# A retention layer with a gated feed-forward on one core: order of the first chunk, place of a weight load, and a split of the first four blocks

## The chip, the cores and the metric

One core of a Trainium2 chip runs the whole program. The metric is device time in microseconds, the median over several executions; less is better. The kernel before took 257.64 us (median of 11, 255.73 to 260.2).

## The reference

Two layers follow each other. The first is retention, a linear attention with a decay per head; the second is an RMS norm and a SwiGLU feed-forward over the tokens.

```python
# q, k, v: (4, 8, 768, 64) float32
gamma = 1.0 - 2.0 ** (-5.0 - np.arange(H))
for t in range(S):
    state = gamma[None, :, None, None] * state + einsum('bhd,bhe->bhde', k[:, :, t], v[:, :, t])
    y[:, :, t] = scale * einsum('bhd,bhde->bhe', q[:, :, t], state)
x = y.transpose(0, 2, 1, 3).reshape(B * S, H * D)          # 3072 tokens x 512
rms = np.sqrt(np.mean(x * x, axis=-1, keepdims=True) + 1e-06)
xn = x / rms * rms_g
g = xn @ w_gate                                            # 512 x 1536
silu = g * (1.0 / (1.0 + np.exp(-g)))
out = silu * (xn @ w_val) @ w_out                          # 1536 x 512
```

## The kernel before

The 768 positions are cut into six chunks of 128 (`c`), and a chunk holds all four batches (`b`): 512 tokens. Per chunk there are an attention part and a feed-forward part. All heads of a batch are worked on together, two heads to a group of 128 rows. Matmuls take bf16 and sum in float32. The decay is put into v (`vdec`) and into the output (`ydec`), so that the state is a plain sum.

**Attention of one batch of a chunk**, in pieces that are placed one by one:

- `cast` (POOL): q and k to bf16, v times decay to `vp`. For chunks 2 to 5 two transposing DMAs on SP (`qT`, `kT`) follow at once.
- T, `piece_t` (chunks 0 and 1): eight transposes on TensorE into `qk_ps`, and one ScalarE copy to `qkT`.
- A, `piece_a`: eight matmuls into two `a_ps` (k against q), and on VectorE the causal mask into `am`, in two halves.
- Y, `piece_y`: `am` times `vp` into `y_ps`, from chunk 1 on the state (`st_b`) times q added to it, and k times `vp` into `kv_ps`; VectorE scales to `x`, ScalarE sums the squares (`xsq`), POOL makes `rstd`. From chunk 1 on VectorE adds `kv_ps` to the state `st_f` and POOL casts it to `st_b`, in two halves of 64 rows. In chunk 0 ScalarE copies it (S, `piece_s`) and POOL casts it in the feed-forward slots 0 to 3 (`piece_sb`).
- N, `piece_n`: VectorE makes `xn`; for chunks 2 to 5 one more transposing DMA on SP writes `xnT`.
- X, `piece_x` (chunks 0 and 1): four transposes on TensorE, and the product with the norm's weight, on ScalarE or VectorE, into `xnT`.

**Feed-forward of a chunk**, in slots: twelve blocks `gv(n)` of eight matmuls of 512 columns (gate and value), a Silu on ScalarE (`sg`) and a product on VectorE (`hT`); then the down projection. In chunk 0 that is twelve quarter slots (`down(b, 4i, 4i+4)`), of which the first four need the first piece of `wo_b` alone, the next four the second, the last four the third; in later chunks four slots of twelve matmuls. ScalarE copies the sum to `o_sb` (three buffers), and SP writes it out.

**What sets the order.** The program is scheduled by hand: each engine and each DMA queue runs in program order. Chunk 0's attention is one written string of steps (lines 374 to 382), with the gate and value weights (W0 to W3) loaded between them on POOL. After that, while chunk c's feed-forward runs, the attention of chunk c+1 is hung into its slots by `PLAN` (chunks 2 to 5) and `PLAN1` (chunk 1): in each slot first the block or down, then the pieces that the plan lists for it, by batch.

Transfers: chunk 0's batch 0 comes over SP, batches 1 to 3 over POOL's queue with a cast on the way (`load0`). Chunk 1's twelve loads stand on SP behind the landing of W1. The three pieces of `wo_b` are issued on POOL ahead of slots 9 (two) and 12. At slot 16 of chunk 0 SP gets the norm's weight (`g_bc`) and the twelve loads of chunk 2, the first of them behind the landing of the second `wo_b` piece:

```python
    WS = {9: (0, 1), 12: (2,)}
...
            if c == 0 and i == 16:
                nc.sync.dma_start(out=g_bc, in_=moe_rms_g.partition_broadcast(128))
                for b in range(B):
                    load(2, b, after=landed["wo", 1])
```

Chunk 0's four outputs are issued on SP after these (slots 20 to 23), and the transposes of chunk 2 after the outputs.

PSUM is split into four banks for attention (`aps`) and four for the feed-forward (`fps`); chunk 0's four `kv_ps` lie in `fps` until S has copied them. Between chunk 0's attention and the feed-forward stand six matmuls without use (`hot`), which keep TensorE busy.

Of the kernel before, what the change touches and what calls it, by code (L numbers as in the profile page):

```python
# [9 lines left out]
F32 = mybir.dt.float32  # L10
BF16 = mybir.dt.bfloat16
AX = mybir.AxisListType
AF = mybir.ActivationFunctionType
ALU = mybir.AluOpType
# [3 lines left out]
def kernel(  # L18
# [77 lines left out]
    for h in range(H):  # L96
# [17 lines left out]
    nc.scalar.activation(warm, zero, AF.Silu)  # L114
    mhalf = const.tile([128, 1], F32, name="mhalf")
    nc.vector.memset(mhalf, -0.5)
    load0(1)
    ident = const.tile([128, 128], BF16, name="ident")
    make_identity(nc, ident)
    load0(2)  # L120
    causal = const.tile([128, 128], BF16, name="causal")
    nc.gpsimd.memset(causal, 1.0)
    nc.gpsimd.affine_select(
        out=causal, in_=causal, compare_op=ALU.is_ge, fill=0.0, base=0,
        pattern=[[1, 128]], channel_multiplier=-1)
    load0(3)

    g_bc = const.tile([128, DM], F32, name="g_bc")


    st_f = [const.tile([128, NHP, D], F32, name=f"st_f{b}") for b in range(B)]
    st_b = [const.tile([128, NHP, 2 * D], BF16, name=f"st_b{b}") for b in range(B)]
    for b in range(B):
        nc.vector.memset(st_b[b], 0.0)
# [55 lines left out]
    def piece_t(c, b):  # L190
        if c > 1:
            return
        if c == 0:
            cur[c, b] = dict(qb=raw0["qb", b], kb=raw0["kb", b])
        d = cur[c, b]
        qk_ps = aps.tile([128, 2, NHP, 128], BF16, name="qk_ps", tag="at")
        for i, n in enumerate(("qb", "kb")):
            for hp in range(NHP):
                nc.tensor.transpose(qk_ps[:, i, hp, :], d[n][:, hp * 128:(hp + 1) * 128], ident)
        qkT = work.tile([128, 2, NHP, 128], BF16, name="qkT")  # L200
        nc.scalar.copy(qkT, qk_ps)
        d["qT"] = qkT[:, 0]
        d["kT"] = qkT[:, 1]

# [15 lines left out]
    def piece_y(c, b):  # L220
# [31 lines left out]
        if c == 0:  # L252
            d["kv"] = kv_ps
        elif c < NCH - 1:
            for i in range(2):
                r = slice(i * 64, i * 64 + 64)
                kv = kv_ps[r, :, i * 64:i * 64 + 64]
                nc.vector.tensor_tensor(out=st_f[b][r], in0=st_f[b][r], in1=kv, op=ALU.add)  # L258
                nc.gpsimd.tensor_copy(st_b[b][r, :, i * 64:i * 64 + 64], st_f[b][r])  # L259

    def piece_s(b):
        for i in range(2):
            r = slice(i * 64, i * 64 + 64)
            nc.scalar.copy(st_f[b][r], cur[0, b]["kv"][r, :, i * 64:i * 64 + 64])

    def piece_sb(b):
        for i in range(2):
            r = slice(i * 64, i * 64 + 64)
            nc.gpsimd.tensor_copy(st_b[b][r, :, i * 64:i * 64 + 64], st_f[b][r])

    def piece_rstd(c, b):
        ms = work.tile([128, 1], F32, name="ms")
# [18 lines left out]
    def piece_x(c, b):  # L291
        d = cur[c, b] if c == 0 else cur.pop((c, b))
        if c > 1:
            return
        xn = d["xn"]
        xt_ps = aps.tile([128, KS, 128], BF16, name="xt_ps", tag="at")
        for s in range(KS):
            nc.tensor.transpose(xt_ps[:, s, :], xn[:, s * 128:(s + 1) * 128], ident)
        if c == 0 and b < B - 1:
            for s in range(KS):  # L300
                nc.scalar.activation(cur[c, "xnT"][:, s, b * C:(b + 1) * C], xt_ps[:, s, :],
                                     AF.Copy, scale=g_col[:, s:s + 1])
            return
        nc.vector.tensor_tensor(  # L304
            out=cur[c, "xnT"][:, :, b * C:(b + 1) * C], in0=xt_ps,
            in1=g_col[:, :, None].to_broadcast([128, KS, 128]), op=ALU.mult)
# [2 lines left out]
        cur[c, "xnT"] = work.tile([128, KS, GT], BF16, name="xnT", bufs=2)  # L309


    PLAN = dict(cast=(0, 1, 2, 3), t=(1, 3, 5, 7), a=(4, 6, 8, 10), y=(5, 7, 9, 11), n=(7, 9, 11, 13), x=(8, 10, 12, 14))

    PLAN1 = dict(cast=(5, 6, 8, 11), t=(7, 9, 11, 17), a=(8, 10, 13, 18), y=(9, 11, 15, 20), n=(11, 13, 17, 22), x=(12, 15, 19, 23))

    def attention(c):
        s = [[] for _ in range(24 if c == 1 else 16)]
# [7 lines left out]


    def ffn(c):
        xnT = cur.pop((c, "xnT"))
        hT = ffw.tile([128, NFF, GT], BF16, name="hT", bufs=2)
        slots = []  # L330

        def gv(n):
            sl = slice(n * 128, (n + 1) * 128)
            g_ps = fps.tile([128, GT], F32, name="g_ps", tag="ff")
            for s in range(KS):
                nc.tensor.matmul(g_ps, wg_b[:, s, sl], xnT[:, s, :], start=s == 0, stop=s == KS - 1)  # L336
            v_ps = fps.tile([128, GT], F32, name="v_ps", tag="ff")
            for s in range(KS):
                nc.tensor.matmul(v_ps, wv_b[:, s, sl], xnT[:, s, :], start=s == 0, stop=s == KS - 1)  # L339
            sg = ffw.tile([128, GT], BF16, name="sg")  # L340
            nc.scalar.activation(sg, g_ps, AF.Silu)  # L341
            nc.vector.tensor_tensor(out=hT[:, n, :], in0=sg, in1=v_ps, op=ALU.mult)  # L342

        o_t = {}

        def down(b, n0=0, n1=NFF):
            if n0 == 0:
                o_t[b] = fps.tile([128, DM], F32, name="o_ps", tag="ff")
            o_ps = o_t[b]
            for n in range(n0, n1):  # L350
                nc.tensor.matmul(o_ps, hT[:, n, b * C:(b + 1) * C], wo_b[:, n, :],  # L351
                                 start=n == 0, stop=n == NFF - 1)
            if n1 < NFF:
                return
            o_sb = ffw.tile([128, DM], F32, name="o_sb")
            nc.scalar.copy(o_sb, o_ps)  # L356
            nc.sync.dma_start(out=out_v[c, b], in_=o_sb)

        for n in range(NFF):
            slots.append(lambda n=n: gv(n))  # L360
        if c == 0:
            for i in range(3):
                for b in range(B):
                    slots.append(lambda b=b, i=i: down(b, 4 * i, 4 * i + 4))
        else:
            for b in range(B):
                slots.append(lambda b=b: down(b))
        return slots


    begin(0)
    P = dict(C=lambda c, b: piece_c(b), V=lambda c, b: piece_v(b), S=lambda c, b: piece_s(b),
             T=piece_t, A=piece_a, Y=piece_y, N=piece_n, X=piece_x, W=lambda c, i: load_w(i))
    for step in ("C0 T0 V0 W0 A0 T1 V1 Y0 W1 A1 T2 V2 N0 Y1 W2 X0 A2 T3 V3 N1 Y2 W3 X1 A3 N2 Y3 X2 S0 S1").split():
        P[step[0]](0, int(step[1]))
    hot = aps.tile([128, GT], F32, name="hot", tag="at")
    for i in range(6):
        nc.tensor.matmul(hot, ident, cur[0, 3]["qT"].rearrange("p a b -> p (a b)"), start=True, stop=True)
    piece_s(2)
    piece_s(3)  # L380
    piece_n(0, 3)
    piece_x(0, 3)
    for b in range(B):
        load(1, b, after=landed["w", 1] if b == 0 else None)

    WS = {9: (0, 1), 12: (2,)}
    for c in range(NCH):
        f_slots = ffn(c)
        a_slots = attention(c + 1) if c + 1 < NCH else [[] for _ in range(16)]
        for i, f_slot in enumerate(f_slots):  # L390
            if c == 0:
                for j in WS.get(i, ()):
                    load_wo(j)
            f_slot()
            if c == 0 and i < B:
                piece_sb(i)
            if c == 0 and i == 16:
                nc.sync.dma_start(out=g_bc, in_=moe_rms_g.partition_broadcast(128))
                for b in range(B):
                    load(2, b, after=landed["wo", 1])  # L400
            if 0 < c < NCH - 2 and i in (5, 7, 9, 11):
                load(c + 2, (i - 5) // 2)
            for f in a_slots[i]:
# [29 lines left out]
```

## Time and profile before

| | us |
|---|---|
| median of 11 runs | 257.64 (255.73 to 260.2) |
| the profiled execution's own time | 258.51 |
| its span, first to last instruction | 256.8 |
| TensorE busy | 228.2 (89% of the span) |
| VectorE busy | 128.1 (50%) |
| POOL busy | 95.5 (37%) |
| ScalarE busy | 90.1 (35%) |
| first feed-forward matmul of chunk 0 | 24.66 |
| first feed-forward matmul of chunk 1 | 69.34 |

PE is TensorE (PEld its weight loads), DVE is VectorE, ACT is ScalarE, POOL is GpSimd, SP the engine whose queue issues most transfers; a name with q behind it (SPq) is that engine's sequencer or DMA queue. A row of the timeline has the start in us, the length, the engine, the line of the kernel, the operation, output and inputs by their names in the program, and in brackets how long the engine had been idle before it and what ended the wait. Rows of neighbouring instructions of one kind are merged (x4): the length is then from the first start to the last end. A matmul's recorded length reaches into the next one's, so prices are taken from start to start.

### The profile page before, as it was taken

To read this page: it belongs to the slowest core of one execution; us is meant where nothing else is said; L and a number is where in the kernel's file an instruction comes from. 1 tells how busy PE (TensorE), PEld (TensorE's weight loads), DVE (VectorE), ACT (ScalarE), POOL (GpSimd) and SP (SyncE) were. 2 spreads that over 40 slices of the span, in tenths; PEclk is the share of its full clock that TensorE was granted. 3 is DMA by queue.
4 is the path that set the end of the run, shared out by engine and by line. 5 is a ranking of instruction groups with operands and counts; after the bars stand their busy time and mean duration, and the time that the engine had idled before them with its cause. 6 is when DMAs were issued, how large, how long until landed. Compare 5 with 4: busy or idle time off the path is not lost.

```text
span 256.8 us, 4122 instructions
## 1 busy us (share of the span) xinstructions
PE 228.2 (89%) x1483; PEld 111.2 (43%) x1510; DVE 128.1 (50%) x227; ACT 90.1 (35%) x178; POOL 95.5 (37%) x177
## 2 busy tenths in 40 slices
PE   1767999696859999999999999999999999999993
PEld 0543445353424544444544444444444444444441
DVE  3793336764423898125888036896045772143300
ACT  6477333512322323233243133432333322333221
POOL 8968156372590222960224930244911111000000
PEclk9997999999988999999999999999999999999999
DMA  9999999979984599945999545999354112300022
GB/s 135 180 199 203 204 221 210 147 151 203 224 240 86 122 221 172 204 123 102 156 223 196 145 103 105 192 216 190 102 123 84 20 20 83 125 0 1 0 84 82
DMA packets 108069, 35.94 MB, mean 140 GB/s; under 512 B 99024, under 2 KB 104656, under 8 KB 108048
## 3 DMA queue, kind: packets, MB, share of 16 engines
q1 hardware_dynamic: 95232, 29.37, 58.6%
q0 software_dynamic: 12288, 6.29, 18.4%
q8 instruction: 12, 0.20, 0.3%
q14 instruction: 9, 0.07, 0.2%
q10 hardware_dynamic: 528, 0.00, 0.1%
HBM read 28.58 MB, written 6.29 MB: 136 GB/s over the span
## 4 chain that ended last, share of the span: by engine, by line
PE 64%; DVE 15%; DMA 7%; ACT 5%; issue 4%; POOL 2%; SPq 1%; ACTq 0%; DVEq 0%; POOLq 0%
PE o_ps L351 20%; PE v_ps L339 19%; PE g_ps L336 18%; DVE am L215 5%; DVE hT L342 4%; DMA wo_b<-in_moe_w_out_dram 3%; DMA v_f<-in_v_dram 2%; DVE x L243 2%; ACT sg L341 2%; ACT xsq L247 2%; PE y_ps L228 2%; DMA out_dram<-o_sb 2%; PE a_ps L211 1%; DVE xn L284 1%; DVE xn L288 1%
## 5 line engine op out<-in xcount | busy, mean ns | idle before, releaser
L342 DVE TENSOR_TENSOR hT<-sg,v_ps 128x512 bf16<-128x512 bf16 x72 | 49.4, 687 | 92.0 <-PE v_ps L339 75.0
L339 PE MATMUL v_ps<-xnT,wv_b 128*128 128x512 bf16 x282 | 74.3, 383 | 3.1 <-ACT o_sb L356 2.6
L336 PE MATMUL g_ps<-xnT,wg_b 128*128 128x512 bf16 x275 | 73.6, 383 | 2.1 <-DVE xnT L304 1.7
L351 PE MATMUL o_ps<-wo_b,hT 128*128 128x512 bf16 x281 | 63.8, 379 | 3.8 <-DMA wo_b<-in_moe_w_out_dram 3.3
L341 ACT ACTIVATE sg<-g_ps 128x512 bf16<-128x512 f32 x72 | 42.7, 594 | 58.6 <-PE g_ps L336 55.5
L339 PEld LDWEIGHTS <-wv_b 128*128 128x128 bf16 x288 | 28.4, 99 | 37.4 <-issue 4.1
L273 POOL TENSOR_SCALAR ms<-ssq 128x1 f32<-128x1 f32 x24 | 4.6, 191 | 102.6 <-ACT xsq L247 102.5
L351 PEld LDWEIGHTS <-hT 128*128 128x128 bf16 x288 | 27.6, 98 | 34.9 <-issue 1.8
L336 PEld LDWEIGHTS <-wg_b 128*128 128x128 bf16 x288 | 26.2, 98 | 30.6 <-issue 2.2
L247 ACT ACTIVATE xsq<-x 128x512 f32<-128x512 f32 x24 | 15.1, 630 | 50.7 <-DVE x L243 48.6
L215 DVE TENSOR_TENSOR am<-a_ps,causal 128x512 bf16<-128x512 f32 x48 | 30.8, 683 | 1.5 <-PE a_ps L211 1.3
L356 ACT COPY o_sb<-o_ps 128x512 f32<-128x512 f32 x24 | 14.0, 585 | 47.2 <-PE o_ps L351 38.7
L180 POOL TENSOR_TENSOR vp<-v_f,vdec 128x512 bf16<-128x512 f32 x20 | 20.8, 1038 | 1.4 <-DMA v_f<-in_v_dram 1.4
L228 PE MATMUL y_ps<-vp,am 128*128 128x64 bf16 x192 | 13.1, 198 | 6.1 <-DVE am L215 6.0
L243 DVE TENSOR_TENSOR x<-y_ps,ydec 128x512 f32<-128x512 f32 x24 | 16.4, 682 | 2.6 <-PE y_ps L233 2.5
L228 PEld LDWEIGHTS <-am 128*128 128x128 bf16 x192 | 8.8, 100 | 15.0 <-DVE am L215 13.5
L178 POOL CAST qb<-q_f 128x512 bf16<-128x512 f32 x20 | 12.1, 607 | 7.6 <-DMA q_f<-in_q_dram 7.3
L284 DVE SCALAR_TENSOR_TENSOR xn<-x,rstd,g_bc 128x512 bf16<-128x512 f32 x16 | 12.3, 766 | 4.9 <-POOL rstd L276 4.9
L259 POOL CAST st_b<-st_f 64x256 bf16<-64x256 f32 x32 | 13.9, 434 | 0.9
L276 POOL TENSOR_TENSOR rstd<-ms,mhalf 128x1 f32<-128x1 f32 x24 | 13.3, 554 | 2.0
L258 DVE TENSOR_TENSOR st_f<-st_f,kv_ps 64x256 f32<-64x256 f32 x32 | 13.2, 414 | 0.5
L179 POOL CAST kb<-k_f 128x512 bf16<-128x512 f32 x20 | 12.5, 624 | 2.0 <-PE a_ps L211 1.4
(55 smaller groups left out, 121.3 us busy)
## 6 DMA issues: line engine op xcount, KB each, us to landing
out_dram<-o_sb SPq DMA_DIRECT2D x24, 256.0 KB, 2.2
q_f<-in_q_dram SPq DMA_DIRECT2D x21, 256.0 KB, 4.6
k_f<-in_k_dram SPq DMA_DIRECT2D x21, 256.0 KB, 4.8
v_f<-in_v_dram SPq DMA_DIRECT2D x21, 256.0 KB, 5.1
wg_b<-in_moe_w_gate_dram POOLq DMA_DIRECT2D x4, 384.0 KB, 9.1
wv_b<-in_moe_w_val_dram POOLq DMA_DIRECT2D x4, 384.0 KB, 10.1
wo_b<-in_moe_w_out_dram POOLq DMA_DIRECT2D x3, 512.0 KB, 7.9
v_f<-in_v_dram POOLq DMA_DIRECT2D x3, 256.0 KB, 6.2
```

What stands on the lines that cost most here:

```text
L180: nc.gpsimd.tensor_tensor(out=vp, in0=v_f, in1=vdec[:, c, :, None].to_broadcast([128, H, D]), op=ALU.mult)
L215: nc.vector.tensor_tensor(out=am[:, i], in0=a_ps[i], in1=causal[:, None, :].to_broadcast([128, NHP, 128]), op=ALU.mult)
L228: nc.tensor.matmul(y_ps[:, h, :], d["am"][:, i, hp, :], d["vp"][:, h, :], start=first, stop=last, skip_group_check=True)
L243: nc.vector.tensor_tensor(out=x, in0=y_ps, in1=ydec[:, c, :, None].to_broadcast([128, H, D]), op=ALU.mult)
L247: nc.scalar.activation(xsq, x.rearrange("p h d -> p (h d)"), AF.Square, accum_out=ssq)
L284: nc.vector.scalar_tensor_tensor(out=xn, in0=x, scalar=d["rstd"], in1=g_bc, op0=ALU.mult, op1=ALU.mult)
L336: nc.tensor.matmul(g_ps, wg_b[:, s, sl], xnT[:, s, :], start=s == 0, stop=s == KS - 1)
L339: nc.tensor.matmul(v_ps, wv_b[:, s, sl], xnT[:, s, :], start=s == 0, stop=s == KS - 1)
L341: nc.scalar.activation(sg, g_ps, AF.Silu)
L342: nc.vector.tensor_tensor(out=hT[:, n, :], in0=sg, in1=v_ps, op=ALU.mult)
L351: nc.tensor.matmul(o_ps, hT[:, n, b * C:(b + 1) * C], wo_b[:, n, :], start=n == 0, stop=n == NFF - 1)
L356: nc.scalar.copy(o_sb, o_ps)
```

## The change

- POOL issues the loads of batches 1 to 3 after `ident` and `causal` are built, not between.
- The string of steps of chunk 0 is reordered; batch 0's and 3's copies of `qkT` are split, half on ScalarE and half on VectorE; batch 2's X goes to VectorE; three `hot` matmuls instead of six; batch 3's X moves into the feed-forward.
- The state `st_f` is kept 128 wide, so that one instruction copies or adds it instead of two; the cast to `st_b` takes the two diagonal halves out of it.
- In chunk 0, blocks 0 to 3 run on the first three batches (384 columns); batch 3's X follows block 1, and after block 3 the four blocks are done for batch 3 (128 columns each) in one bank each for gate and value.
- In `PLAN` (chunks 2 to 5) Y stands two slots behind A, with N behind it; from slot 12 on the pieces of a slot run ahead of the down projection. `PLAN1` moves chunk 1's pieces up by one to four slots.
- The three pieces of `wo_b` are issued ahead of slots 8 (two) and 9, and chunk 2's loads stand behind the third piece instead of the second.
- `o_sb` has five buffers instead of three.
- The very last down projection is done in two halves of 256 columns, copied by ScalarE and VectorE and written from the queues of SP and ScalarE.

```diff
-    load0(1)
     ident = const.tile([128, 128], BF16, name="ident")
     make_identity(nc, ident)
-    load0(2)
     causal = const.tile([128, 128], BF16, name="causal")
...
-    load0(3)
+    for b in range(1, B):
+        load0(b)
...
-    st_f = [const.tile([128, NHP, D], F32, name=f"st_f{b}") for b in range(B)]
+    st_f = [const.tile([128, NHP, 2 * D], F32, name=f"st_f{b}") for b in range(B)]
...
-        nc.scalar.copy(qkT, qk_ps)
+        if c == 0 and b in (0, B - 1):
+            nc.scalar.copy(qkT[:, 0], qk_ps[:, 0])
+            nc.vector.tensor_copy(qkT[:, 1], qk_ps[:, 1])
+        else:
+            nc.scalar.copy(qkT, qk_ps)
...
         elif c < NCH - 1:
-            for i in range(2):
-                r = slice(i * 64, i * 64 + 64)
-                kv = kv_ps[r, :, i * 64:i * 64 + 64]
-                nc.vector.tensor_tensor(out=st_f[b][r], in0=st_f[b][r], in1=kv, op=ALU.add)
-                nc.gpsimd.tensor_copy(st_b[b][r, :, i * 64:i * 64 + 64], st_f[b][r])
+            nc.vector.tensor_tensor(out=st_f[b], in0=st_f[b], in1=kv_ps, op=ALU.add)
+            piece_sb(b)
 
     def piece_s(b):
-        for i in range(2):
-            r = slice(i * 64, i * 64 + 64)
-            nc.scalar.copy(st_f[b][r], cur[0, b]["kv"][r, :, i * 64:i * 64 + 64])
+        nc.scalar.copy(st_f[b], cur[0, b]["kv"])
...
-        if c == 0 and b < B - 1:
+        if c == 0 and b < B - 2:
...
-    PLAN = dict(cast=(0, 1, 2, 3), t=(1, 3, 5, 7), a=(4, 6, 8, 10), y=(5, 7, 9, 11), n=(7, 9, 11, 13), x=(8, 10, 12, 14))
-    PLAN1 = dict(cast=(5, 6, 8, 11), t=(7, 9, 11, 17), a=(8, 10, 13, 18), y=(9, 11, 15, 20), n=(11, 13, 17, 22), x=(12, 15, 19, 23))
+    PLAN = dict(cast=(0, 1, 2, 3), t=(1, 3, 5, 7), a=(4, 6, 8, 10), y=(6, 8, 10, 12), n=(8, 10, 12, 13), x=(8, 10, 12, 14))
+    PLAN1 = dict(cast=(4, 5, 7, 9), t=(6, 8, 10, 12), a=(7, 9, 11, 14), y=(8, 10, 12, 16), n=(10, 12, 14, 19), x=(11, 13, 15, 20))
...
+        def gv(n0, n1=None, t=slice(0, GT)):
+            n1 = n0 + 1 if n1 is None else n1
+            w = t.stop - t.start
+            g_ps = fps.tile([128, n1 - n0, w], F32, name="g_ps", tag="ff")
+            v_ps = fps.tile([128, n1 - n0, w], F32, name="v_ps", tag="ff")
+            for ps, w_b in ((g_ps, wg_b), (v_ps, wv_b)):
+                for n in range(n0, n1):
+                    for s in range(KS):
+                        nc.tensor.matmul(ps[:, n - n0, :], w_b[:, s, n * 128:(n + 1) * 128], xnT[:, s, t],
+                                         start=s == 0, stop=s == KS - 1)
+            sg = ffw.tile([128, n1 - n0, w], BF16, name="sg")
             nc.scalar.activation(sg, g_ps, AF.Silu)
+            nc.vector.tensor_tensor(out=hT[:, n0:n1, t], in0=sg, in1=v_ps, op=ALU.mult)
+
+        EARLY = 4
+        early = slice(0, GT - C)
+
+        def gv_first(n):
+            gv(n, t=early)
+            if n == 1:
+                piece_x(0, B - 1)
+            if n == EARLY - 1:
+                gv(0, EARLY, slice(GT - C, GT))
...
+        def down_last(b):
+            o_sb = ffw.tile([128, DM], F32, name="o_sb", bufs=5)
+            for i in range(2):
+                m = slice(i * (DM // 2), (i + 1) * (DM // 2))
+                o_ps = fps.tile([128, DM // 2], F32, name="o_ps", tag="ff")
+                for n in range(NFF):
+                    nc.tensor.matmul(o_ps, hT[:, n, b * C:(b + 1) * C], wo_b[:, n, m],
+                                     start=n == 0, stop=n == NFF - 1)
+                (nc.scalar.copy if i == 0 else nc.vector.tensor_copy)(o_sb[:, m], o_ps)
+                (nc.sync if i == 0 else nc.scalar).dma_start(out=out_v[c, b][:, m], in_=o_sb[:, m])
...
-            o_sb = ffw.tile([128, DM], F32, name="o_sb")
+            o_sb = ffw.tile([128, DM], F32, name="o_sb", bufs=5)
...
-    for step in ("C0 T0 V0 W0 A0 T1 V1 Y0 W1 A1 T2 V2 N0 Y1 W2 X0 A2 T3 V3 N1 Y2 W3 X1 A3 N2 Y3 X2 S0 S1").split():
+    for step in ("C0 T0 V0 W0 A0 T1 V1 Y0 W1 A1 T2 V2 Y1 W2 N0 A2 T3 X0 V3 Y2 W3 S0 N1 A3 S1 X1 Y3 N2 X2 S2").split():
...
-    for i in range(6):
+    for i in range(3):
...
-    piece_s(2)
     piece_s(3)
     piece_n(0, 3)
-    piece_x(0, 3)
...
-    WS = {9: (0, 1), 12: (2,)}
+    WS = {8: (0, 1), 9: (2,)}
...
+            if i >= NFF and c > 0:
+                for f in a_slots[i]:
+                    f()
+                a_slots[i] = []
             f_slot()
...
-                    load(2, b, after=landed["wo", 1])
+                    load(2, b, after=landed["wo", 2])
```

More of the change, by code (lines that the diff above doesn't have):

```diff
@@ L268, in piece_sb @@
             r = slice(i * 64, i * 64 + 64)
-            nc.gpsimd.tensor_copy(st_b[b][r, :, i * 64:i * 64 + 64], st_f[b][r])
+            nc.gpsimd.tensor_copy(st_b[b][r, :, i * 64:i * 64 + 64], st_f[b][r, :, i * 64:i * 64 + 64])
     def piece_rstd(c, b):
@@ L327, in ffn @@
     def ffn(c):
-        xnT = cur.pop((c, "xnT"))
+        xnT = cur[c, "xnT"]
         hT = ffw.tile([128, NFF, GT], BF16, name="hT", bufs=2)
         slots = []
[L332 to L342, printed above, removed]
@@ L359, in ffn @@
         for n in range(NFF):
-            slots.append(lambda n=n: gv(n))
+            slots.append(lambda n=n: gv_first(n) if c == 0 and n < EARLY else gv(n))
         if c == 0:
@@ L366, in ffn @@
             for b in range(B):
-                slots.append(lambda b=b: down(b))
+                slots.append(lambda b=b: down_last(b) if (c, b) == (NCH - 1, B - 1) else down(b))
         return slots
```

## The prediction

> **What bounds the kernel now.** I read the page's head, then the stretches cut at stage borders, then the timeline of the one stretch that is out of line.
>
> ```profile
> span 256.8 us, 4122 instructions
> DMA  9999999979984599945999545999354112300022
> ...
> 50.12:69.34 19.22, 14.30 (x119) 7.65 (x121) 10.70 (x20) 5.69 (x11) 8.77 (x18) 1.00 1.05 192
> 69.34:82.55 13.21, 10.53 (x39) 4.26 (x41) 2.75 (x4) 3.37 (x6) 7.61 (x11) 0.87 0.77 178
> 110.60:147.80 37.20, 36.11 (x237) 17.43 (x241) 21.16 (x36) 12.06 (x24) 14.96 (x29) 1.00 0.88 156
> ```
>
> In the stretches the first two numbers are the length and TensorE's busy time, the third from the end is the granted clock. A settled chunk (110.60 to 147.80) takes 37.2 us and TensorE is full. Chunk 0's down projections with chunk 1's attention (50.12 to 69.34) leave it 4.9 us idle, and the first five blocks of chunk 1 take 13.21 us. The DMA row is 9 for the first 51 us: until then transfers, not engines, set what can end. The rows around that border, in order of time:
>
> ```profile
> 44.10 1.59 POOL L154 DMA_DIRECT2D wo_b<-in_moe_w_out_dram  x2
> 51.70 1.04 PE L351 MATMUL o_ps<-wo_b,hT 128*128 128x512 bf16 x4 [1.58 <-DMA wo_b<-in_moe_w_out_dram]
> 54.21 0.37 SPq L64 DMA_DIRECT2D q_f<-in_q_dram  x1
> 55.52 0.83 POOL L154 DMA_DIRECT2D wo_b<-in_moe_w_out_dram  x1
> 57.27 1.93 SPq L64 DMA_DIRECT2D k_f<-in_k_dram  x1
> 63.08 0.87 SPq L64 DMA_DIRECT2D q_f<-in_q_dram  x1
> 63.46 1.02 PE L351 MATMUL o_ps<-wo_b,hT 128*128 128x512 bf16 x4 [1.70 <-DMA wo_b<-in_moe_w_out_dram]
> 68.71 1.07 SPq L64 DMA_DIRECT2D v_f<-in_v_dram  x1
> 69.34 1.04 PE L336 MATMUL g_ps<-xnT,wg_b 128*128 128x512 bf16 x4 [0.79 <-DVE xnT L304]
> 69.87 1.56 SPq L357 DMA_DIRECT2D out_dram<-o_sb  x2
> 71.05 0.88 SPq L357 DMA_DIRECT2D out_dram<-o_sb  x2
> 74.09 0.59 ACT L356 COPY o_sb<-o_ps 128x512 f32<-128x512 f32 x1 [6.58 <-DMA out_dram<-o_sb]
> 74.73 1.53 PE L339 MATMUL v_ps<-xnT,wv_b 128*128 128x512 bf16 x4 [2.62 <-ACT o_sb L356]
> 75.13 1.32 SPq L187 DMA_TRANSPOSE qT<-qb  x1
> 76.54 1.21 SPq L187 DMA_TRANSPOSE kT<-kb  x1
> 82.55 0.40 PE L211 MATMUL a_ps<-qT,kT 64*128 64x128 bf16 x8
> DMA to landing us min/median/max: 7.6/7.9/9.3
> DMA to landing us min/median/max: 2.4/2.4/4.4
> ```
>
> Chunk 0 waits for the first piece of wo (51.70) and for the third (63.46). Chunk 1 starts at 69.34, late by xnT. ScalarE's fourth output copy then finds no o_sb buffer free until an output has landed (6.58 us), because the outputs stand on SP behind the twelve loads of chunk 2 (the last issued at 68.71). So TensorE stands 2.62 us. The transposes of chunk 2 stand on SP behind the fourth output (75.13), and chunk 2's first A comes at 82.55. The last two rows are the landings, from the issue, of wo_b's three pieces and of kT's transposes in this stage.
>
> The prices of TensorE's pieces:
>
> ```profile
> 38.47 0.39 PE L199 MATMUL qk_ps<-ident,qb 128*128 128x128 bf16 x4
> 38.91 1.03 PE L336 MATMUL g_ps<-xnT,wg_b 128*128 128x512 bf16 x4
> 80.73 1.03 PE L336 MATMUL g_ps<-xnT,wg_b 128*128 128x512 bf16 x4
> 81.59 1.03 PE L339 MATMUL v_ps<-xnT,wv_b 128*128 128x512 bf16 x4
> 82.88 1.04 PE L336 MATMUL g_ps<-xnT,wg_b 128*128 128x512 bf16 x4
> 83.76 1.03 PE L339 MATMUL v_ps<-xnT,wv_b 128*128 128x512 bf16 x4
> 85.33 1.03 PE L336 MATMUL g_ps<-xnT,wg_b 128*128 128x512 bf16 x3
> ```
>
> From start to start: four matmuls of 512 columns 0.86 (80.73 to 81.59), so 0.216 each and 1.73 a block; T, eight transposes, 0.44 (38.47 to 38.91), so 0.055 each and X 0.22; A 82.88-81.59-0.86 = 0.43; Y 85.33-83.76-0.86 = 0.71.
>
> **Part 1: the prologue and the first four blocks, costed at nothing.**
>
> ```profile
> 4.26 0.24 POOL masks.py:197 MEMSET ident<- 128x128 bf16 x1
> 4.58 0.35 POOL masks.py:199 TENSOR_SCALAR_AFFINE_SELECT ident<-ident 128x128 bf16<-128x128 bf16 x1
> 24.66 1.02 PE L336 MATMUL g_ps<-xnT,wg_b 128*128 128x512 bf16 x4 [0.88 <-DVE xnT L304]
> ```
>
> Ident and causal, two such pairs on POOL (2 x 0.59 = 1.2 us), now run ahead of the nine loads of batches 1 to 3, whose rows come that much later; batch 0's, alone on the DMA engines meanwhile, come sooner. VectorE gets two half copies of qkT and batch 2's xnT more, and loses nothing; eight state copies become four of the shape at 74.09 (0.59). Block 0 needs three batches instead of four, so I put its start at 23 (an estimate; ends 22 and 24.7). Its four blocks at 384 columns cost 32 x 0.75 x 0.216 = 5.2, the fourth batch 32 x 0.055 = 1.8: 7.0 against 6.9. With A2, X0 and X3 moved ahead (0.87) and three hot matmuls fewer, TensorE reaches its first down near 49.5 instead of 50.12. That gains nothing: the first wo piece is issued on POOL behind chunk 1's third cast, whose rows arrive as before (44.10), so the down still starts at 51.7. This wait covers all of Part 1, half clock in the first blocks included; over 2 us would have to be lost there to show. What can show is that POOL's loads start 1.2 us later on engines busy throughout: 0 to 1.2, I take 0.5, since batch 0's rows use the engines meanwhile. First down 52.2.
>
> **Part 2: from the first down to chunk 1.** Left are twelve quarter downs (12 x 0.86 = 10.4), two Y, one T, one A and three X (1.42+0.44+0.43+0.66 = 2.95) and an estimated 0.4 of gaps: 13.7. wo's third piece is issued on POOL behind the rstd and st_b of batch 0's Y (an estimate of 47.5) instead of at 55.52, and follows the second on its queue. The first two landed at 51.7 and 44.9+9.3 = 54.2, 2.5 us apart; so the third lands at 56.7, with the 0.5 at 57.2. Its use comes eight quarters and 2.7 of attention later, at 61.8: the wait of 1.70 goes. Batch 3's Y, n and x end by slot 20, so xnT isn't late either. Chunk 1 starts at 52.2+13.7 = 65.9, 3.4 us sooner.
>
> **Part 3: chunk 1 to chunk 2's first A.** With five o_sb buffers the 2.62 us go, and the half clock behind them: 0.87 in a stretch of 13.21 us is 3.4 us at half speed. TensorE would reach A after five blocks, at 74.6. But kT is late next. On SP, chunk 2's loads now wait for wo's third piece: 57.2 instead of 54.21. The twelve issues took 69.78-54.21 = 15.6 us with wo between them; undisturbed, the first four took 3.1 (54.21 to 57.27) and the last six 6.7 (63.08 to 69.78), which makes 3.1+8x1.12 = 12.0: end 69.2 (72.8 at the old pace). Then four outputs, 2.5 us (three took 69.87 to 71.93), q's transpose at 71.7, k's at 73.1, landed 2.4 to 4.4 later: 75.5 to 77.5. I take 76.0, near the median. A moves from 82.55 to 76.0: **-6.5 us**, with a new TensorE wait of 1.4 ahead of it. The later transposes, one pair per 2.6 us, keep ahead of an A every 4.6.
>
> **Part 4: two slots between A and Y, chunks 2 to 5.**
>
> ```profile
> 86.19 1.03 PE L339 MATMUL v_ps<-xnT,wv_b 128*128 128x512 bf16 x4
> 87.51 0.69 DVE L342 TENSOR_TENSOR hT<-sg,v_ps 128x512 bf16<-128x512 bf16 x1 [0.56 <-ACT sg L341]
> 88.11 1.28 DVE L215 TENSOR_TENSOR am<-a_ps,causal 128x512 bf16<-128x512 f32 x2
> 90.10 0.74 DVE L284 SCALAR_TENSOR_TENSOR xn<-x,rstd,g_bc 128x512 bf16<-128x512 f32 x1
> 91.36 0.86 DVE L258 TENSOR_TENSOR st_f<-st_f,kv_ps 64x256 f32<-64x256 f32 x2
> 100.45 10.52 PE L351 MATMUL o_ps<-wo_b,hT 128*128 128x512 bf16 x47
> ```
>
> From the end of block 6 (87.05) to the first down TensorE took 13.4 us; five blocks, three A and three Y are 12.07: 1.33 us of waiting. It doesn't vanish: am of batch 3 stands in VectorE's order behind the same hT, xn, x and st_f as before, now packed into slot 10. VectorE's pace here: hT 0.60, am 1.39, xn with x 1.26, st_f as one 128x512 an estimated 0.65. In the new order, counted from the end of block 6, it waits for block 8 until 4.9, then does hT, xn, x, st_f, am, two hT, xn, x, st_f, am: 13.3. TensorE would reach batch 3's Y at 12.1 and ends it at 13.95, with batch 0's Y (0.71) inside, against 13.4+0.71 before: 0.16 sooner, three times; for the last attention, which has no state update, I take 0.4. **-0.9 us**; ends: +4 (am a microsecond later in each of four chunks) and -5 (all waits gone).
>
> **Part 5: the tail.**
>
> ```profile
> out_dram<-o_sb SPq DMA_DIRECT2D x24, 256.0 KB, 2.2
> ```
>
> The last copy of 0.59 becomes one of half the width on VectorE (0.43, half of the st_f pair), and its output has half the bytes (0 to half of 2.2 saved, I take 0.25): **-0.4**. Its 24 matmuls of half width cost what 12 cost.
>
> Sum: -6.5-0.9-0.4 = -7.8: span 249.0. The profiled execution took 258.51 for its 256.8, 0.87 above the median of the runs; on the median, 257.64-7.8 = 249.8.
>
> **The clock, row against page.** The wait of 2.62 us was followed by half clock, those of 1.58 and 1.70 by none (1.00 in their stretch). The new wait of 1.4 (0.9 to 2.9) lies at that border. The Trainium skill (TensorE: Matmul & The Clock Gate, What's actually happening) has the clock fall after an idle window of about 3.4 us; by that the new wait is free at any length in question, and the sum is 249.8 without rival (a). The trace does not agree: 2.62 us sufficed.
>
> **Rivals.** (a) The new wait drops the clock: 3.4 us at half speed lose 1.7: 251.5. For it, the 0.87; against, the wait is likely under 1.7. (b) wo's third piece is held on POOL until about 55.5 as before, or chunk 2's loads keep their pace of 15.6 us: A at 79.6 to 82, 253.4 to 255.8. For it, POOL works in order and the rstd there waits on ScalarE; against, only one Y stands before it. (c) Slower: the same hold, longer. Each us that wo lands after 57.2 is a us on A; at 65.0 the gain of 7.8 is spent, from 66.3 the kernel is over 0.5% slower. An issue at 59 with the landing of 7.9 gives 66.9: 259.5. Against: batch 0's Y would have to end some twelve us after its slot. (d) All waits of Part 4 go (245.7), or kT is there at 74.6 (248.4). (e) The change moves waits only: if A stays at 82.55, what is left is 256.3.
>
> **How the numbers follow.** 0.5% (1.3 us) is about what a measurement of this kernel can tell from no change. Forecast 0.55, (a) 0.13, (b) 0.12, (d) 0.10, (e) 0.06, (c) 0.04. Faster: forecast, (a), (b), (d), 0.90. The range leaves out (c), (e), the late half of (b) and the early end of (d), some 0.2: 246.8 to 254.0.
>
> **What would show it.** Right: the first down waits for wo near 52; chunk 1 starts near 66; no ScalarE wait for an output; SP's first transpose near 72; chunk 2's first A near 76, behind a TensorE wait; in later chunks Y of batch 3 alone waits for am. Wrong: the third wo piece issued after 50 on POOL, half clock after 76, or settled chunks that differ from 37 us by over 0.5.

## The result, and the profile after

The changed kernel takes 251.47 us, median of 12 runs (250.5 to 253.92). The kernel before, over the 11 runs that the prediction had and 36 more beside these, takes 256.56 (255.66 to 260.2). The ratio is 0.9795, interval 0.9769 to 0.9822: 2.05% faster. The forecast of 249.8 was 1.6 us too low. The profiled execution of the changed kernel took 251.68 us, for a span of 249.9.

From the page of the changed kernel, its head and its DMA row:

```profile
span 249.9 us, 4173 instructions
DMA  8999999997997599944999455999354014200022
```

Two stretches, from where TensorE gets to the first down to chunk 1, and on to chunk 2's first A (length, TensorE's busy time; third from the end the granted clock, as a share of full speed):

```profile
51.47:66.41 14.94, 13.30 (x106) 7.30 (x109) 9.81 (x16) 4.10 (x8) 7.05 (x16) 1.00 1.03 181
66.41:78.14 11.73, 8.79 (x40) 3.79 (x39) 3.44 (x5) 3.57 (x6) 6.02 (x8) 1.00 1.19 237
```

The first takes 14.94 us instead of 19.22; TensorE gets there 1.35 later and waits that much less for wo, so the first down starts at 51.70 in both kernels. The five first blocks of chunk 1 take 11.73 instead of 13.21, at full clock, but TensorE is busy in only 8.79 of them. The DMA row hardly differs: the start is nearly as full as it was.

The length of a settled chunk is best taken from first A to first A. Before:

```profile
119.54 0.40 PE L211 MATMUL a_ps<-qT,kT 64*128 64x128 bf16 x8
156.60 0.40 PE L211 MATMUL a_ps<-qT,kT 64*128 64x128 bf16 x8
```

and after:

```profile
114.90 0.40 PE L215 MATMUL a_ps<-qT,kT 64*128 64x128 bf16 x8
151.65 0.40 PE L215 MATMUL a_ps<-qT,kT 64*128 64x128 bf16 x8
```

That is 37.06 before (the 37.20 of the prediction has its borders slightly off) and 36.75 after, 0.31 less.

The rows of the border, in order of time:

```profile
23.94 1.49 PE L340 MATMUL g_ps<-xnT,wg_b 128*128 128x384 bf16 x4
47.68 0.95 POOL L154 DMA_DIRECT2D wo_b<-in_moe_w_out_dram  x1
51.00 0.40 PE L215 MATMUL a_ps<-qkT 64*128 64x128 bf16 x8 [0.46 <-ACT qkT L205]
51.70 0.81 PE L375 MATMUL o_ps<-wo_b,hT 128*128 128x512 bf16 x3 [0.30 <-DMA wo_b<-in_moe_w_out_dram]
53.42 0.20 PE L232 MATMUL y_ps<-vp,am 128*128 128x64 bf16 x1 [0.92 <-DVE am L219]
57.58 0.37 SPq L64 DMA_DIRECT2D q_f<-in_q_dram  x1
66.41 1.03 PE L340 MATMUL g_ps<-xnT,wg_b 128*128 128x512 bf16 x4
66.61 0.59 ACT L380 COPY o_sb<-o_ps 128x512 f32<-128x512 f32 x1 [0.28 <-PE o_ps L375]
69.01 1.08 SPq L64 DMA_DIRECT2D v_f<-in_v_dram  x1
70.18 3.59 SPq L381 DMA_DIRECT2D out_dram<-o_sb  x4
73.86 1.44 SPq L187 DMA_TRANSPOSE qT<-qb  x1
75.40 1.21 SPq L187 DMA_TRANSPOSE kT<-kb  x1
78.14 0.40 PE L215 MATMUL a_ps<-qT,kT 64*128 64x128 bf16 x8 [2.94 <-DMA kT<-kb]
```

wo's third piece is issued at 47.68, and no down waits for it. Chunk 1 starts at 66.41 instead of 69.34. ScalarE's fourth output copy finds a buffer at once. What is new stands in the last row: TensorE waits 2.94 us for chunk 2's first kT. The queue of SP shows why: loads up to 70, then four outputs for 3.59 us, and only then the transposes. So A comes 4.4 us earlier than before, and chunk 1's earlier start would have allowed 7.3.

### The profile page after: what moved, and what is told of

It reads as the page before. It is cut to its first block, busy times and chain, and to the rows that moved or that the text cites. A ratio compares the mean times of both kernels' runs of the same rounds, so it can differ in the third digit from the quotient of the medians.

```text
span 249.9 us, 4173 instructions
## 1 busy us (share of the span) xinstructions
PE 226.5 (91%) x1524; PEld 116.3 (47%) x1551; DVE 127.3 (51%) x216; ACT 87.6 (35%) x171; POOL 95.5 (38%) x177
## 4 chain that ended last, share of the span: by engine, by line
PE 67%; DMA 12%; DVE 6%; SPq 6%; POOL 5%; issue 3%; ACT 1%; DVEq 0%; POOLq 0%
PE o_ps L375 23%; PE g_ps L340 19%; PE v_ps L340 18%; DMA v_f<-in_v_dram 7%; SPq L64 6%; DMA wv_b<-in_moe_w_val_dram 4%; DVE am L219 2%; PE a_ps L215 2%; PE y_ps L232 2%; PE y_ps L237 1%; DVE xn L283 1%; DMA kT<-kb 1%; PE o_ps L365 1%; POOL wo_b L154 1%; PE kv_ps L244 1%
## 5 line engine op out<-in xcount | busy, mean ns | idle before, releaser
L344 DVE TENSOR_TENSOR hT<-sg,v_ps 128x512 bf16<-128x512 bf16 (+1 forms) x73 | 49.6, 679 | 90.0 <-PE v_ps L340 84.7
L340 PE MATMUL v_ps<-xnT,wv_b 128*128 128x512 bf16 (+2 forms) x297 | 73.7, 369 | 0.5
L340 PE MATMUL g_ps<-xnT,wg_b 128*128 128x512 bf16 (+2 forms) x293 | 73.7, 371 | 0.4
L343 ACT ACTIVATE sg<-g_ps 128x512 bf16<-128x512 f32 (+1 forms) x73 | 42.9, 588 | 63.3 <-PE g_ps L340 58.3
L375 PE MATMUL o_ps<-wo_b,hT 128*128 128x512 bf16 x268 | 60.6, 379 | 0.6 <-DMA wo_b<-in_moe_w_out_dram 0.3
L340 PEld LDWEIGHTS <-wv_b 128*128 128x128 bf16 x304 | 29.3, 98 | 33.5 <-issue 0.5
L340 PEld LDWEIGHTS <-wg_b 128*128 128x128 bf16 x304 | 27.6, 98 | 30.5 <-issue 0.8
L375 PEld LDWEIGHTS <-hT 128*128 128x128 bf16 x276 | 26.5, 98 | 30.5 <-issue 0.3
L251 ACT ACTIVATE xsq<-x 128x512 f32<-128x512 f32 x24 | 15.1, 630 | 49.9 <-DVE x L247 47.5
L268 POOL CAST st_b<-st_f 64x256 bf16<-64x256 f32 x40 | 17.1, 429 | 1.3
L259 DVE TENSOR_TENSOR st_f<-st_f,kv_ps 128x512 f32<-128x512 f32 x16 | 10.8, 676 | 0.0
```

Source lines behind the costliest of these rows:

```text
L251: nc.scalar.activation(xsq, x.rearrange("p h d -> p (h d)"), AF.Square, accum_out=ssq)
L340: nc.tensor.matmul(ps[:, n - n0, :], w_b[:, s, n * 128:(n + 1) * 128], xnT[:, s, t], start=s == 0, stop=s == KS - 1)
L344: nc.vector.tensor_tensor(out=hT[:, n0:n1, t], in0=sg, in1=v_ps, op=ALU.mult)
```

## The experiments

Every ratio is to the kernel before, in runs on the same chip (its medians there: 256.75 us for runs 1 to 4, 256.67 for 5 to 8, 256.86 for 9 to 12). Runs 1 to 4, 5 to 8 and 9 to 12 were on three different chips, so across these groups the ratios compare better than the medians. "The change" is the changed kernel, 0.9795 [0.9769, 0.9822].

**1. Are the output buffers the change?** The kernel before, with five o_sb buffers and nothing else:

```
-            o_sb = ffw.tile([128, DM], F32, name="o_sb")
+            o_sb = ffw.tile([128, DM], F32, name="o_sb", bufs=5)
```

> The kernel before with one edit: five o_sb buffers. Theory (the change's gain is the unblocking of the SP queue at the border of chunks 0 and 1, and chunk 0's edits add nothing to it): no ScalarE wait for an output, the fourth output issued near 72 and the first transpose near 72.5 instead of 75.13, TensorE from 69.34 through five blocks without a wait, first A of chunk 2 at 78.0 to 78.5 where the change has 78.14. That is -4.2 against before, 252.3, and what is left to the change (about 0.9) is the plan of the later chunks and the tail. Rival (moving wo up and the new order in chunk 0 carry it): the buffers alone give back at most the wait of 2.62, 254.

256.27 us, ratio 0.9953 [0.9924, 0.9982]. Its border:

```profile
63.77 1.02 PE L351 MATMUL o_ps<-wo_b,hT 128*128 128x512 bf16 x4 [2.40 <-DMA wo_b<-in_moe_w_out_dram]
69.65 1.04 PE L336 MATMUL g_ps<-xnT,wg_b 128*128 128x512 bf16 x4 [0.79 <-DVE xnT L304]
78.39 0.40 PE L211 MATMUL a_ps<-qT,kT 64*128 64x128 bf16 x8
```

In this execution the 2.62 us and the half clock behind them are gone, and A comes at 78.39 with no wait: as early as in the change, by another way, and as the theory had it. But over 12 runs the buffers alone bring half a per cent, and both expected times, 252.3 and 254, were missed. The profiled execution took 254.53, 1.7 less than the median. It and one of 254.22 are the two with a granted clock of 1.00, and the two shortest; the other ten, at 0.976 to 0.993, took 254.91 to 258.32. Which waits their clock fell behind wasn't traced.

**2. The change without the buffers.**

```
-            o_sb = ffw.tile([128, DM], F32, name="o_sb", bufs=5)
+            o_sb = ffw.tile([128, DM], F32, name="o_sb", bufs=3)
```

(in both places)

> The changed kernel with o_sb back at three buffers. Theory: chunk 1 still starts at 66.4, but the fourth copy waits for the first output, which stands on SP behind chunk 2's loads until 70.2 and lands at 74; TensorE stands about 5 us from 69, the clock drops, first A at 82 to 83 instead of 78.14: 255.5 to 256. Rival (earlier wo and the earlier start of chunk 1 carry it): A moves by 1 at most, 252.5.

256.34 us, 0.996 [0.9937, 0.9983].

```profile
74.26 0.59 ACT L380 COPY o_sb<-o_ps 128x512 f32<-128x512 f32 x1 [6.45 <-DMA out_dram<-o_sb]
74.89 1.86 PE L340 MATMUL v_ps<-xnT,wv_b 128*128 128x512 bf16 x4 [4.26 <-ACT o_sb L380]
82.37 0.40 PE L215 MATMUL a_ps<-qT,kT 64*128 64x128 bf16 x8
```

The old wait is back, and on TensorE longer (4.26 us for 2.62), because chunk 1 starts earlier (67.89 in this execution, 69.34 before) and meets the same landing. A is at 82.37, where it was before the change. So the change needs the buffers (without them 1.65% of the time, 4.2 us, is lost again), and almost all else in it has to pass through them.

**3. The change without early blocks.** Blocks 0 to 3 on all four batches, X3 in the prologue, six hot matmuls as before.

```
-            slots.append(lambda n=n: gv_first(n) if c == 0 and n < EARLY else gv(n))
+            slots.append(lambda n=n: gv(n))
...
-    for i in range(3):
+    for i in range(6):
...
+    piece_x(0, 3)
```

> The changed kernel with blocks 0 to 3 at four batches again: batch 3's X in the prologue, six hot matmuls. Theory: the feed-forward starts 1 to 2 us later, and nothing of it reaches the end, because wo's landing (51.7) and then kT's landing (78.1, with 2.94 us of waiting before A) stand behind it: 251.5 within 0.6, A at 78 to 78.4. Rival (the split of the first four blocks is a part of the gain): 253 or more.

250.94 us, 0.9782 [0.9734, 0.9829]: the same as the change.

```profile
25.40 1.02 PE L340 MATMUL g_ps<-xnT,wg_b 128*128 128x512 bf16 x4 [0.78 <-DVE xnT L303]
51.53 1.02 PE L375 MATMUL o_ps<-wo_b,hT 128*128 128x512 bf16 x4 [0.20 <-DMA wo_b<-in_moe_w_out_dram]
76.83 0.40 PE L215 MATMUL a_ps<-qT,kT 64*128 64x128 bf16 x8 [1.70 <-DMA kT<-kb]
```

The first block starts 1.46 us later than in the change, and the first down comes at the same time: the early blocks, which the title names, gain nothing. A came 1.3 us sooner than in the change, against the expected 78 to 78.4: in this execution SP's loads ended 0.7 sooner and the four outputs took 2.90 us instead of 3.59.

**4. Outputs of chunk 0 from ScalarE's queue**, so that SP's transposes don't stand behind them.

```
-            nc.sync.dma_start(out=out_v[c, b], in_=o_sb)
+            (nc.scalar if c == 0 else nc.sync).dma_start(out=out_v[c, b], in_=o_sb)
```

> The changed kernel with chunk 0's four outputs issued from ScalarE's queue, so that the transposes of chunk 2 follow its loads on SP at once. Theory (A waits for the transposes, these for their turn on SP): first transpose near 70.2 instead of 73.86, kT near 74.5, A at 75.0 to 75.5 where TensorE gets to it: -3, 248.5. Rival (kT is late because the DMA engines are still at chunk 2's rows, not because of the queue): kT lands as late as before, 251.5.

256.83 us, 0.9983 [0.9954, 1.0011]: both expectations failed, and the whole gain of the change is gone.

```profile
70.45 0.34 ACTq L381 DMA_DIRECT2D out_dram<-o_sb  x1
70.83 0.58 ACT L380 COPY o_sb<-o_ps 128x512 f32<-128x512 f32 x1 [3.23 <-DMA v_f<-in_v_dram]
75.03 0.34 ACTq L381 DMA_DIRECT2D out_dram<-o_sb  x1
75.41 1.09 ACT L343 ACTIVATE sg<-g_ps 128x512 bf16<-128x512 f32 x2 [4.00 <-DMA v_f<-in_v_dram]
76.06 1.87 PE L340 MATMUL g_ps<-xnT,wg_b 128*128 128x512 bf16 x4 [3.57 <-ACT sg L343]
```

The transposes did move forward (the first at 70.95), but now ScalarE did nothing for 3.23 and 4.00 us, most of it just ahead of the issue of an output, and TensorE stood behind it. The trace names the landing of chunk 2's v rows as what it stood for; the program has no such dependence, so why an issue stands there isn't settled. Since ScalarE's standing hides it, this run can't tell whether SP's order holds A.

**5. The old PLAN** for chunks 2 to 5, and the pieces behind the downs again:

```
-    PLAN = dict(..., y=(6, 8, 10, 12), n=(8, 10, 12, 13), ...)
+    PLAN = dict(..., y=(5, 7, 9, 11), n=(7, 9, 11, 13), ...)
...
-            if i >= NFF and c > 0:
-                for f in a_slots[i]:
-                    f()
-                a_slots[i] = []
```

> The changed kernel with the old plan for chunks 2 to 5 (one slot between A and Y, pieces behind the down). Theory (VectorE's order sets it, so two slots move the wait rather than remove it): batches 1 to 3 each wait 0.2 to 0.6 us for am again, chunks longer by 0.2 to 0.5 and the last attention's by 1: 252.3 to 253. Rival (the two slots take the waits out and are the larger part of the gain): 255 or more.

253.21 us, 0.9847 [0.9805, 0.989], a little above the expected 252.3 to 253: 0.5%, or 1.3 us, is the plan's share; the intervals overlap a little, so the size is rough. The trace agrees: from first A to first A a chunk takes 36.96 to 37.00 again, as before the change.

**6. One slot more for batch 3.** In the change, from chunk 2's attention on, only batch 3's Y still waits for am. Its rows in chunk 2's attention, with the am that they wait for:

```profile
93.81 1.28 DVE L219 TENSOR_TENSOR am<-a_ps,causal 128x512 bf16<-128x512 f32 x2
94.55 0.20 PE L232 MATMUL y_ps<-vp,am 128*128 128x64 bf16 x1 [0.47 <-DVE am L219]
95.15 0.38 PE L232 MATMUL y_ps<-vp,am 128*128 128x64 bf16 x7 [0.40 <-DVE am L219]
```

The experiment puts a quarter of the downs between that A and its Y:

```
-    PLAN = dict(..., y=(6, 8, 10, 12), n=(8, 10, 12, 13), ...)
+    PLAN = dict(..., y=(6, 8, 10, 13), n=(8, 10, 12, 14), ...)
```

> The changed kernel with batch 3's Y in slot 13 instead of 12, behind one down projection, and N in 14 (chunks 2 to 5). Theory: the 0.87 us that TensorE waits for am ahead of that Y in each of four chunks go, as a down stands between; xnT of batch 3 comes 2.6 us later, still before the next chunk's first block or at its border: -2.5 to -3.5, 248 to 249. Rival (the wait comes back at the next chunk's first block, for xnT behind two outputs on SP): 251 to 252.

**247.96 us (246.8 to 249.12), 0.9638 [0.9596, 0.968]**: faster than both kernels, and about as expected.

```profile
78.34 0.40 PE L215 MATMUL a_ps<-qT,kT 64*128 64x128 bf16 x8 [4.36 <-DMA kT<-kb]
...
95.81 2.75 PE L375 MATMUL o_ps<-wo_b,hT 128*128 128x512 bf16 x12
98.40 0.40 PE L232 MATMUL y_ps<-vp,am 128*128 128x64 bf16 x8
...
115.58 0.40 PE L215 MATMUL a_ps<-qT,kT 64*128 64x128 bf16 x8
...
151.12 0.40 PE L215 MATMUL a_ps<-qT,kT 64*128 64x128 bf16 x8
```

The first 12 downs don't need am, so they cover it, and Y runs its eight matmuls without a stop. The stretch 142 to 178, in the change and then in this kernel:

```profile
142.00:178.00 36.00, 34.88 (x234) 17.28 (x237) 20.48 (x32) 12.06 (x24) 14.06 (x28) 1.00 0.90 161
```

```profile
142.00:178.00 36.00, 36.00 (x244) 17.86 (x243) 20.57 (x32) 12.05 (x24) 15.24 (x29) 1.00 0.87 163
```

TensorE is busy for all of the 36 us instead of 34.88. From first A to first A a chunk takes 35.54 (115.58 to 151.12); in the change it was 36.75 (114.90 to 151.65). That is 1.2 us in each of three chunks and 0.8 from the last chunk's first A on, some 4.4 in all, of which this execution, the slowest of its six (249.12 us), gave 1.7 back to half clock behind the 4.36 us wait at 78.34.

**7. wo late again**, and chunk 2's loads behind its second piece:

```
-    WS = {8: (0, 1), 9: (2,)}
+    WS = {9: (0, 1), 12: (2,)}
...
-                    load(2, b, after=landed["wo", 2])
+                    load(2, b, after=landed["wo", 1])
```

> The changed kernel with wo's pieces ahead of slots 9, 9 and 12 as before, and chunk 2's loads behind the second piece as before. Theory (A of chunk 2 is set by loads, outputs and transposes on SP, and these take the same engines whichever goes first): wo's third piece issued near 52.7 and landed near 61, at most 1 us of waiting for it, chunk 2's last load near 69.8 and A near 77.5 as in the change: 251 to 252. Rival (the earlier third piece is what moves chunk 1 up and carries the gain): 253.5 or more.

250.37 us, 0.9733 [0.9689, 0.9778].

```profile
71.33 1.33 SPq L187 DMA_TRANSPOSE qT<-qb  x1
75.28 0.40 PE L215 MATMUL a_ps<-qT,kT 64*128 64x128 bf16 x8 [1.23 <-DMA kT<-kb]
```

Moving wo up earns nothing; by the medians it costs about 1 us, with overlapping intervals. It is a little less than the expected 251 to 252. In this profile, the shortest of its six (248.81), the transposes come 2.5 us sooner and A 2.9.

**8. Chunk 0's outputs behind the transposes of batches 0 and 1**, still on SP:

```
+    late = []
...
-            nc.sync.dma_start(out=out_v[c, b], in_=o_sb)
+            if c == 0:
+                late.append((b, o_sb))
+            else:
+                nc.sync.dma_start(out=out_v[c, b], in_=o_sb)
...
+            if c == 1 and i == 1:
+                for b, o in late:
+                    nc.sync.dma_start(out=out_v[0, b], in_=o)
```

> The changed kernel with chunk 0's four outputs issued on SP behind the transposes of chunk 2's batches 0 and 1 (slot 1 of chunk 1). The run with outputs on ScalarE's queue could not tell, since ScalarE stood 4 us at each issue. Theory (turn on SP): first transpose near 70.2, kT landed near 74.5, A at 75.1 to 75.5 with little waiting: -2.5 to -3, 248.5 to 249. Rival (kT is late because the DMA engines are busy with chunk 2's rows): A stays at 77.5 to 78.2, 251 to 251.5.

250.34 us, 0.9719 [0.9678, 0.976]: 1 to 2 us for the change's 2.94 us wait, a smaller gain than the expected 248.5 to 249.

```profile
53.70 0.20 PE L233 MATMUL y_ps<-vp,am 128*128 128x64 bf16 x1 [1.05 <-DVE am L220]
68.33 1.03 PE L341 MATMUL g_ps<-xnT,wg_b 128*128 128x512 bf16 x4
70.16 1.79 SPq L188 DMA_TRANSPOSE qT<-qb  x1
77.06 0.40 PE L216 MATMUL a_ps<-qT,kT 64*128 64x128 bf16 x8
```

kT is in time and A waits for nothing. It is only 1.1 us sooner in this execution, because chunk 1 started 1.9 us later, behind a stretch at half clock, which shows in this row (granted clock 0.83 in 10 us, 3.4 us at half speed):

```profile
50.00:60.00 10.00, 8.09 (x66) 4.70 (x65) 5.73 (x10) 3.34 (x7) 3.60 (x9) 0.83 0.87 155
```

kT's transpose is issued at 72.05 instead of 75.40, so SP's order was the main cause of the wait. It wasn't all of it: in run 11, which has the same order, TensorE reaches A at 74.19 and still waits 0.81 for kT. In run 8's execution, what decided when A came was the clock ahead of chunk 1.

**9. Chunk 1's plan and wo both as before**, the rest of the change kept (the plan's pieces move by one to five slots):

```
-    PLAN1 = dict(cast=(4, 5, 7, 9), ..., y=(8, 10, 12, 16), n=(10, 12, 14, 19), x=(11, 13, 15, 20))
+    PLAN1 = dict(cast=(5, 6, 8, 11), ..., y=(9, 11, 15, 20), n=(11, 13, 17, 22), x=(12, 15, 19, 23))
```

and the two edits of run 7.

> The changed kernel with chunk 1's old plan, wo's old places and chunk 2's loads behind the second piece: what is left of the change is five o_sb buffers, the prologue with the early blocks, the later chunks' plan and the tail. Against the run with wo late it differs by chunk 1's plan alone (250.4). Theory (chunk 1's pieces moved up are what starts chunk 1 three us earlier, and they take away the waits on the way that drop the clock): chunk 1 starts at 69 to 70, A at 78 to 79 without a wait for kT, 252.5 to 254. Rival (A is held by kT in any case, so chunk 1's plan adds nothing): 250 to 251.

250.8 us, 0.9793 [0.9746, 0.984]: the rival was right, and the expectation of a loss wrong.

```profile
61.90 1.02 PE L375 MATMUL o_ps<-wo_b,hT 128*128 128x512 bf16 x4 [1.43 <-DMA wo_b<-in_moe_w_out_dram]
67.78 1.04 PE L340 MATMUL g_ps<-xnT,wg_b 128*128 128x512 bf16 x4 [0.79 <-DVE xnT L303]
76.52 0.40 PE L215 MATMUL a_ps<-qT,kT 64*128 64x128 bf16 x8
```

The waits for wo (1.43) and xnT (0.79) are back and chunk 1 starts 1.4 us later than in the change, but A comes at 76.52, without a wait and sooner than the change's 78.14. In these two executions the time won ahead of chunk 1 was handed back, all of it, at kT.

**10 to 12. Do the good edits add up?** Run 10 has the edits of 8 and 6; run 11 moves chunk 1's third Y to slot 13 besides (n 15, x 16); run 12 adds wo late, as in 7.

> The changed kernel with both edits that helped: chunk 0's outputs behind two pairs of transposes, and batch 3's Y in slot 13. Theory (they sit in different stretches and add): A of chunk 2 where TensorE gets to it (75 to 77, by what the clock does at 52 to 58), no wait for am from chunk 2 on: 245.5 to 247. Rival (the clock falls after another wait and takes it back): 248.

248.37 us, 0.9694 [0.9656, 0.9733].

> The run before it with chunk 1's batch 2 also one slot later (Y in 13, N in 15, X in 16), so that a down projection stands between wo's landing and this Y. Theory: the 1.4 us that TensorE waits for am there go, and with them the half clock that followed at 54.7 in the run with late outputs; since A no longer waits for kT, all of it reaches the end: 1.4 to 3 less than the run before, 244 to 245.5. Rival (kT, landing near 75, holds A again): 246 to 247.

249.2 us, 0.9709 [0.9675, 0.9743].

> The run before it with wo's old places and chunk 2's loads behind the second piece, which brought A forward by 2.9 us in the run with wo late alone. Theory: chunk 2's transposes start near 67.5, so kT is there before TensorE, but A is TensorE's by now, and the third wo piece lands later (a wait at slot 20 of up to 1): no gain, 244.5 to 246. Rival (kT still binds): 1 us or more below the run before it.

247.51 us (246.0 to 249.01), 0.9656 [0.9616, 0.9697]. All three lie within the interval of run 6 or a little above: nothing adds to it. All three missed the expected times by 1.4 us or more; only the rivals of 10 (248) and 12 (1 us or more below run 11) came near. The wait had moved one chunk on; in run 12:

```profile
74.27 0.40 PE L216 MATMUL a_ps<-qT,kT 64*128 64x128 bf16 x8
...
103.31 1.71 PE L341 MATMUL g_ps<-xnT,wg_b 128*128 128x512 bf16 x4 [2.06 <-DMA xnT<-xn]
```

A is 3.9 us earlier than in the change, and chunk 2's first block then waits 2.06 us for the transposed xn of its last batch (2.26 in run 10, 3.16 in run 11).

## Why the prediction was right, and where not

**The sum.** Predicted were -7.8 us for the profiled executions; they differ by 258.51-251.68 = 6.8. That this is so near is in part luck: the border (Part 3) gave 2.1 less than forecast, and Parts 4 and 5 together gave 1.2 more. Subtracting the sum from the median of before was the worse step: the profiled execution of before stood 1.95 above the median of all 47 runs, and that of after only 0.21 above its own. So a profiled difference of 6.8 is 5.1 between medians. Of the 1.6 by which the forecast missed (251.47 for 249.84), 1.0 is the sum and 1.7 this difference in standing, less the 1.1 by which the median of before itself fell from 257.64 to 256.56 with more runs. The prediction gave the 0.87 above the median but took nothing off for it. The half clock of that execution doesn't explain its standing by itself: its mean granted clock was 0.985, and of the 51 executions of the kernel before that stood beside the experiments the 11 at 0.983 to 0.988 have a median of 256.7, the 28 at 0.989 to 0.994 one of 257.0. What else made it long is open.

**Part 1, costed at nothing: held.** The blocks started at 23.94 (23 forecast, inside 22 to 24.7), the first down was 0.5 early (51.7 for 52.2), and run 3 shows no gain from the early blocks. The cover was thin, though: TensorE was there at 51.4, not 49.5, having begun 0.94 later than forecast and waited 0.46 for qkT, and only 0.30 was left of the wait for wo. The 0.5 put down for POOL's later loads did not show.

**Part 2, chunk 1 at 65.9: 0.5 off.** From the first down (51.70) it took 14.71 for 13.7, which the earlier first down half hides; am held TensorE 0.92 at 53.42 and 0.39 more in the same Y, where 0.4 stood for all gaps. The third piece of wo came when forecast (47.68 for 47.5), and rivals (b) and (c), which needed it held, fell with that; so did the other condition of (b), since chunk 2's loads took 12.5 us (57.58 to 70.09) and not 15.6.

**Part 3, -6.5: the mis-sized term.** It measured -4.4. The mechanism is as told: no wait for an output, and kT late next, behind SP's queue. Three durations were small: the loads began 0.4 later and ended at 70.1 for 69.2; four outputs took 3.59 us for the 2.5, which was worked out from three that took 2.06; and with that the transposes came at 73.86 for 71.7. The TensorE wait is 2.94 for 1.4. Part of this is one execution's scatter: with the same order on SP the four outputs took 2.90, 3.77 and 2.81 us in runs 3, 5 and 6, and A came at 76.83, 77.06 and 78.34, all later than 76.0. Runs 8 and 9 show the cause: with SP's order changed, or the transposes sooner, A did not wait. Run 2 shows that the term needs the buffers. In run 1's profile they carry all of it by themselves, but not in its median.

**Part 4, -0.9: under-sized.** After A the profile gained 2.5 us, 0.6 of it in the tail, so 1.9 in the chunks: 0.23 to 0.31 in each of three, where 0.16 was forecast, and 1.1 from the last chunk's first A (193.59 before, 188.41 after) to TensorE's end, where 0.4 was. Run 5's trace, with the old plan, has the old lengths back, so this is the plan's; by its ratio the plan is worth 1.3. That am would be late for batch 3 alone was right, and run 6 shows what that left: 3.5 us by the medians, 4.0 by the ratios, more than all of Part 4. The prediction named that wait and stopped at its sign.

**Part 5, -0.4: 0.6 in the profile,** not tried alone. The last matmuls:

```profile
243.76 2.67 PE L365 MATMUL o_ps<-wo_b,hT 128*128 128x256 bf16 x23
```

TensorE ends at 246.43 and the span at 249.9, 3.5 later; before it was 4.1.

**Rival (a)**, the clock falling behind the new wait, did not happen in the profile (1.00 in every stretch). The argument against it was that the wait would be under 1.7; it was 2.94, and the clock held all the same, so that (a) did not come was luck. The time of (a), 251.5, is what was measured, for other reasons: the later kT, and where the profiled execution of before stood.

**What stays open.** Between the kernel with buffers alone (0.9953) and run 9 (0.9793) lie the order of the prologue with its split copies, the wide state, the early blocks, PLAN and the tail. PLAN and the tail account for about 2 us of the 4, the early blocks for none; that the remaining 2 come from the order of chunk 0's loads and steps is argued from chunk 1's start (69.65 in run 1, 67.78 in run 9). Neither that order nor the wide state was tried alone.

## What to carry to other kernels

When a stage starts earlier, look at the queue that feeds the next one: here chunk 1 started 3.2 us sooner than with the buffers alone (66.41 for 69.65 in run 1), and chunk 2's first A only 0.25 (78.14 for 78.39). The rest was lost at transposes that stand on SP behind twelve loads and four outputs, and once those were sooner, a wait came one chunk on, at xnT. A short wait that comes back in every chunk (1.2 us, by the length of a chunk) was worth more, and cheaper to take away by one number in a table, than the large one at a border. And before subtracting a profiled gain from a median, ask how far the profiled execution stands above it.

## What the runs showed of the hardware

**The clock doesn't follow the length of one wait.** TensorE waited 2.94 us in the change at 78.14, 3.04 in run 5, 3.16 in run 11 and 2.40 in run 1, and the clock stayed full; after 4.36 (run 6), 2.62 (before) and 2.06 (run 12) it was halved for 3.4 us, and in run 8 near a wait of 1.05. The stretches of run 6 and of run 12 around these waits:

```profile
79.00:83.00 4.00, 4.00 (x13) 1.45 (x12) 1.75 (x3) 0.60 (x1) 0.00 (x0) 0.59 0.50 98
```

```profile
94.00:110.00 16.00, 13.94 (x58) 5.79 (x57) 2.81 (x4) 4.09 (x8) 10.36 (x16) 0.89 0.98 201
```

The Trainium skill (TensorE: Matmul & The Clock Gate, What's actually happening) tells of a free-running window of about 3.4 us and has the clock fall after one idle window or more. The half-clock stretches agree with that length, being 3.4 us, or 6.8 as in run 4 after 74.4; that a whole window must be idle does not agree, at 2.06. The place of a wait against the window would fit this; no run here moved it alone. Of the changed kernel's twelve runs, ten lie within 250.5 to 251.7 us, and of these six had a granted clock of 0.977 to 0.980 and four of 0.993 to 1.00, with no difference in time. That would fit if what the clock lost in the six lay beside another wait; they weren't traced, so this is not shown.

**The time that an issue takes isn't fixed.** In the change the outputs of 256 KB took 0.9 us each of SP behind the loads (3.59 for four), and 0.33 at the tail, where no loads are left and the 16 DMA engines' share reads 0.29 (239 to 246.5) instead of 1.19 (66.41 to 78.14); from ScalarE's queue the issue itself is 0.34, but the engine did nothing for 3 to 4 us around it (run 4). That the traffic makes the difference is likely from these places, and was not tried by itself.
